# A replanned order for attention with adapters: paired stores, stores cut in unequal parts, and stores that wait on loads

## Chip, core and metric

The kernel runs on one core of a Trainium2 chip. The metric is the device time of one execution in microseconds: 254.63 us as the median of three runs before the change (254.41 to 254.83). The profiled execution took 254.46 us; the program's own span in it is 252.7 us.

## What is computed

Four batches of 6400 rows with 256 channels. First, attention across channels: the 256 x 256 product of normalised k and q over all rows, softmax, and v times the result. Then each row of that result gets a low-rank update from the best 2 of 8 adapters. Cut to what matters:

```python
# q, k, v: (4, 6400, 256) fp32
qn = q / (norm(q, axis=1) + 1e-6);  kn = k / (norm(k, axis=1) + 1e-6)
s = kn.transpose(0, 2, 1) @ qn / tau          # per batch 256 x 256
a = softmax(s);  x = (v @ a).reshape(25600, 256)
logits = x @ w_gate                            # 8 experts
top 2 of the logits, w = softmax of the two
out = x + sum over the two of w * ((x @ A[e]) @ B[e])     # rank 16
```

## The kernel before, in words

**Tiling.** A batch's 6400 rows lie as 128 partitions x 50 columns; one column is 128 rows of 256 fp32. q and k come in pieces of 17, 17 and 16 columns (some cut smaller at the start and in batch 3), v in five pieces of 10 columns, all by GpSimd's queue (L578), which casts to bf16 on the way. The first 4 columns of q and k and the weights come by the queues of SP and ACT. Buffers: 6 pieces of q/k, 3 of v, 4 of transposed v (vT), 7 of output (y), 6 PSUM banks.

**Stages of a batch.** For each column the Gram step G multiplies k by q into the accumulators (L593), and k by k and q by q for the norms (L597, L602). For groups of columns named in OFF the norms go another way: ScalarE squares (L615), VectorE adds (L621), and one small matmul (n2p, L636) sums over partitions. When all 50 columns are in, a chain of small steps follows (norms, rq, s, exp, aT, waA, a), whose end gives the softmax matrix a and a times the gate and A weights. Then each piece of v is transposed (T, L788), and goes through the gate. A piece in MERGED does logits and A product in one matmul group (ZL, L812); the others do logits first (log, L826) and the A product later (Z, L879). gzT (L902) transposes the gated product, Y (L915 and L920) adds v times a and the adapter, Ye (L769 on ScalarE, L771 on VectorE) copies Y out of PSUM into a y piece, and a store (L928) on SP's queue writes the piece. The last two pieces of batch 3 are stored in 4, 4 and 2 columns each.

**Order.** Nothing of the order is left to a scheduler at run time. `make_plan` lists all steps with their engine times, what they need, and what buffers they take and give. `Plan.run` plays them through once at build time with a model of the engines, the TensorE clock and the DMA queues, and the order that comes out is the order of each engine's instructions. WORDS is the order of loads, AHEAD and SQ shift ranks.

**Held stores.** A store of a piece in HOLD does not start before a named load has landed. In this kernel the hold is a small DMA of its own: SP waits for the load, then copies 16 elements into `scrap` (L645), and the stores after it wait on SP's list. SP's list is in order, so a store that waits keeps back all stores behind it, and their y pieces with them.

Of the kernel before, what the change touches and what calls it, by code (L numbers as in the profile page):

```python
# [18 lines left out]
class Step:  # L19
# [3 lines left out]
    def __init__(self, key, eng, deps, rank, take, give, size=0.0):  # L23
        self.packet = max(size, 0.08)
        self.key, self.eng, self.deps, self.rank = key, eng, deps, rank
        self.take, self.give, self.size = take, give, size
        self.users, self.place = [], {}
        self.ready, self.end, self.on = 0.0, None, None
        self.left = len(deps)
        self.only = next(iter(eng)) if len(eng) == 1 else None  # L30


class Clock:


    WINDOW, FIRST, LOW, HIGH = 3.413, 0.31, 0.5, 0.8
# [29 lines left out]
    SPARE = 1.0  # L66


class Plan:

    LAT = 0.07
    DMA_LAT = 1.8
    ENGINES = ("PE", "DVE", "ACT", "POOL", "SP")
    ISSUE = 0.55
    ISSUE_LAT = 1.8
    STORE_LAT = 1.4
    OUT = 8

# [15 lines left out]

    def run(self, head):
# [4 lines left out]
        loads, queue, stores = list(self.loads), [], []  # L100
        now, out, left = 0.0, 0, sum(s.key[0] != "warm" for s in self.steps.values())
        free["POOL"] = 0.2
        clock = Clock()

# [5 lines left out]
        def can_take(s):  # L110
            return all((kind, name) in held or self.store[kind] for kind, name in s.take)

        def start(s, eng):
            for kind, name in s.take:
                if (kind, name) not in held:
                    held[kind, name] = self.store[kind].pop(0)
                    s.place[kind] = held[kind, name]
            s.on = eng
            s.t = now
            self.out.append(s)  # L120

# [5 lines left out]
        while left:  # L127
            again = False
            if (loads and free["POOL"] <= now + 1e-9 and out < self.OUT and can_take(loads[0])):
                s = loads.pop(0)  # L130
                start(s, "POOL")
                out += 1
                free["POOL"] = now + self.ISSUE
                push(free["POOL"], "free", None)
                push(now + self.ISSUE_LAT, "asked", s)
                again = True
            for e in self.ENGINES:
# [3 lines left out]
                for s in wait[e]:  # L141
                    if not can_take(s) or (s.key[0] == "warm" and not clock.idle(now)):
                        continue
# [3 lines left out]
                    if best is None or (s.rank, s.seq) < (best.rank, best.seq):  # L147
                        best = s
# [9 lines left out]
                else:  # L158
                    push(free[e], "end", best)
# [3 lines left out]
            busy = [x for x in (queue, stores) if x]  # L163
            t = events[0][0] if events else float("inf")
            base = max(now, head)

            share = sum(x[0].packet for x in busy)
            if busy:
                t = min(t, base + min(x[0].size / x[0].packet for x in busy) * share)
            assert t < float("inf"), [s.key for s in self.steps.values() if s.end is None][:20]  # L170
            if t > base:
                for x in busy:
                    x[0].size -= (t - base) * x[0].packet / share
                    if x[0].size < 1e-6:
                        push(t + self.DMA_LAT, "landed", x[0])
                        out -= x is queue
                        x.pop(0)
            now = max(now, t)
            while events and events[0][0] <= now + 1e-9:
                _, _, what, s = heapq.heappop(events)  # L180
                if what == "asked":
                    queue.append(s)
                elif what == "store":
                    stores.append(s)
# [3 lines left out]
                elif what == "landed":  # L188
                    push(now + (SAFE if s.on == "POOL" else 0.0), "end", s)
                    for u in s.users:  # L190
                        if u.key[0] == "hold":
                            u.left -= 1
                            if u.left == 0:
                                push(now, "ready", u)
                elif what == "end":
# [6 lines left out]
                    for u in s.users:  # L202
                        u.left -= u.key[0] != "hold"
                        if u.left == 0 and u.eng and u.key[0] != "hold":
                            push(now + (0.0 if s.on == u.only else self.LAT), "ready", u)
# [5 lines left out]
NC = 50  # L211
# [4 lines left out]
V = ((0, 1), (1, 1), (2, 1), (3, 1), (4, 1))  # L216
# [13 lines left out]

def make_plan(B, order, ahead):
# [6 lines left out]
    for kind, b, i in order:  # L238
        if kind == "v":
            p.add(("load", "v", b, i, V[i][0] * PC, V[i][1] * PC), {}, (), 0, take=(("v", (b, i)),),  # L240
                  size=LOAD * V[i][1] * PC + 0.062)
            continue
        for c, n in PARTS.get((b, i), QK[i:i + 1]):
            for h in "qk":
                p.add(("load", h, b, i, c, n), {}, (), 0, take=(("qk", (h, b, i)),), size=LOAD * n + 0.062)

    for h in "qk":
        p.add(("cast", h), {"ACT": 0.6}, [("load", h, 0, 0) + PARTS[0, 0][0]], 0)
    p.loads[2].size += 0.5
    for b in range(B):  # L250

        for i, (c0, n) in enumerate(QK):
            for c in range(c0, c0 + n):
# [8 lines left out]
                p.add(("G", b, c), {"PE": 0.442 - 0.112 * sum((b, group_of(c), w) in OFF for w in "kq")}, deps,  # L262
# [4 lines left out]
        for w in "kq":  # L267
# [5 lines left out]
            for x, g in enumerate(halves):  # L273
                c, n = GROUPS[g]
                i = max(i for i, q in enumerate(QK) if q[0] <= c)
                p.add(("sq", w, b, g), {"ACT": 0.2 + 0.2125 * n},
                      [k for k in p.steps if k[:4] == ("load", w, b, i) and k[4] < c + n and c < k[4] + k[5]]
                      + [("cast", w)] * ((b, c) == (0, 0)), pos["qk", b, i] - SQ, take=(("ssq", (w, b)) if x == 0 else ("sq", (w, b, g)),),
                      give=(("qk", (w, b, i)),))
                if x:  # L280
                    p.add(("add", w, b, g), {"DVE": 0.15 + 0.268 * n},
# [4 lines left out]
            if halves:  # L286
                p.add(("red", w, b), {"DVE": 1.9}, [before], pos["qk", b, len(QK) - 1] - 1, give=(("ssq", (w, b)),))
                p.add(("n2p", w, b), {"PE": 0.35}, [("red", w, b), ("G", b, NC - 3)], -100, take=(("bank", ("n2p", w, b)),))
                late.append(w)
        if b == 0:  # L290
            p.add(("wts",), {"DVE": 1.8}, [("load", "k", 0, len(QK) - 1) + PARTS[0, len(QK) - 1][1]], -200)
# [3 lines left out]
        p.add(("accs", b, 1), {"ACT": 0.38}, [end], ch)  # L295
        p.add(("n2", b, 0), {"DVE": 0.45}, [end], ch)
        p.add(("accs", b, 0), {"ACT": 0.38}, [("n2", b, 0)], ch)
        p.add(("n2", b, 1), {"DVE": 0.45}, [("accs", b, 1)], ch)
        p.add(("rsqrt", b), {"DVE": 1.9 + 0.2 * len(late)},
              [("n2", b, 0), ("n2", b, 1)] + [("n2p", w, b) for w in late], ch, take=(("port", b),),  # L300
              give=(("port", b),) + tuple(("bank", ("n2p", w, b)) for w in late))
        p.add(("rq_ps", b), {"PE": 0.45}, [("rsqrt", b)], ch, take=(("bank", ("rq", b)),))
        for ic in range(2):
            p.add(("s", b, ic), {"DVE": 0.42}, [("rq_ps", b), ("accs", b, ic)], ch, give=(("bank", ("rq", b)),))
            p.add(("exp", b, ic), {"ACT": 0.68}, [("s", b, ic)], ch)
            p.add(("aT_ps", b, ic), {"PE": 0.14}, [("exp", b, ic)], ch, take=(("bank", ("aT", b)),))
        p.add(("recip", b), {"DVE": 0.17}, [("exp", b, 0), ("exp", b, 1)], ch)
        p.add(("aT", b), {"DVE": 0.42}, [("aT_ps", b, 0), ("aT_ps", b, 1)], ch, give=(("bank", ("aT", b)),))
        p.add(("waA_ps", b), {"PE": 0.35}, [("aT", b), ("wts",)], ch, take=(("bank", ("waA", b)),))
        p.add(("waA", b, 0), {"DVE": 0.35}, [("waA_ps", b), ("recip", b)], ch, give=(("bank", ("waA", b)),))  # L310
        p.add(("waA", b, 1), {"ACT": 0.38}, [("waA_ps", b), ("recip", b)], ch, give=(("bank", ("waA", b)),))
        p.add(("a", b), {"DVE": 0.5}, [("recip", b), ("aT", b)] + [("a", b - 1)] * (b > 0), ch + 1)

        for i in range(NP):
            v = max(g for g, (i0, _) in enumerate(V) if i0 <= i)
            x = pos["v", b, v] + 0.3 * (i - V[v][0])
            for u, (c, n) in enumerate(UNITS):
                p.add(("T", b, i, u), {"PE": 0.112 * n + 0.01}, [("load", "v", b, v, V[v][0] * PC, V[v][1] * PC)], x - ahead,
                      take=(("vT", (b, i)), ("bank", ("T", b, i, u))),
                      give=(("v", (b, v)),) if u == len(UNITS) - 1 else ())  # L320
                p.add(("Te", b, i, u), {"DVE": 0.16 + 0.125 * n, "ACT": 0.17 + 0.213 * n},
                      [("T", b, i, u)], x - ahead, give=(("bank", ("T", b, i, u)),))
            merged = (b, i) in MERGED
            if merged:
                for z, (c, n) in enumerate(ZUNITS):
                    p.add(("ZL", b, i, z), {"PE": 0.1145 * n + 0.005},
                          [("Te", b, i, u) for u, (c0, n0) in enumerate(UNITS) if c0 < c + n and c < c0 + n0]
                          + [("waA", b, ic) for ic in range(2)], x - ahead,
                          take=(("bank", ("ZL", b, i, z)), ("zl", (b, i))))
                    p.add(("ZLe", b, i, z), {"ACT": 0.17 + 0.1145 * n, "DVE": 0.14 + 0.142 * n},  # L330
                          [("ZL", b, i, z)], x - ahead, give=(("bank", ("ZL", b, i, z)),))
                prev = [("ZLe", b, i, z) for z in range(len(ZUNITS))]
            else:
                p.add(("log", b, i), {"PE": 0.55},
                      [("Te", b, i, u) for u in range(len(UNITS))] + [("waA", b, ic) for ic in range(2)], x - ahead,
                      take=(("bank", ("log", b, i)), ("gate", (b, i))))
                p.add(("loge", b, i), {"ACT": 0.27, "DVE": 0.27}, [("log", b, i)], x - ahead,
                      give=(("bank", ("log", b, i)),))
                prev = [("loge", b, i)]
            for name, eng, t in (("m1", "DVE", .27), ("eq1", "DVE", .27), ("lm", "DVE", .27),  # L340
                                 ("m2", "DVE", .27), ("msum", "DVE", .19), ("t", "DVE", .27),
# [645 lines left out]
```

## Time and profile before

| | |
|---|---|
| time, median of 3 | 254.63 us |
| span of the profiled execution | 252.7 us |
| TensorE busy | 217.8 us (86%), 2357 matmuls |
| VectorE busy | 192.7 us (76%), 528 instructions |
| ScalarE busy | 151.1 us (60%), 269 instructions |
| DMA packets | 11243 |
| out_dram<-y, 1280 KB each | 18, with 16.7 us from issue to landing |
| v<-in_v_dram, 640 KB each | 20, with 20.5 us from issue to landing |

How to read it: the busy share of an engine is an average over the span; TensorE waits for the first loads early and is full later. The page cuts the span into 40 slices of 6.3 us; in the rows of part 2 each digit is the busy share in tenths, and 9 means 90% or more. A load is counted in bytes as it is written (bf16, so half of what is read), a store as it is (fp32). The time from issue to landing is long because a transfer waits in its queue behind others. The chain that ended last is followed back from the last instruction of the compute engines.

### The profile page before, as it was taken

Reading aid. Unit: us, or ns where it says so; the run is one execution under the profiler, and the core shown is the slowest. Engines: PE = TensorE matmul, PEld = TensorE weight load, DVE = VectorE, ACT = ScalarE, POOL = GpSimd, SP = SyncE. Lnnn points to the kernel's source line nnn. Section 1 sums busy time; section 2 is a strip of 40 time slices with the busy share of each in tenths; the row PEclk is TensorE's granted clock in tenths of the full one; section 3 lists DMA queues with packets and bytes.
Section 4 is the critical chain, followed back from the end, with each engine's and each line's share of the span. In section 5 each row is a group of like instructions: output and inputs, shape, how many; then the busy total and the mean of one; then the engine's idle time right before and its main releaser. Section 6 shows DMA issues by size and latency. Waiting matters only on the chain.

```text
span 252.7 us, 5852 instructions
## 1 busy us (share of the span) xinstructions
PE 217.8 (86%) x2357; PEld 193.0 (76%) x2357; DVE 192.7 (76%) x528; ACT 151.1 (60%) x269; POOL 27.1 (11%) x54
## 2 busy tenths in 40 slices
PE   0274995988999998689999999889999979999990
PEld 0162882876999996579899899779999769999980
DVE  0055589869899987588899899489898898889850
ACT  5454427546786543975667768362674846657671
POOL 7003010040002002000500100500000000000000
PEclk9998899999999999999999999999999999999997
DMA  8999999999999999999999999999999999999996
GB/s 251 217 217 209 211 223 208 217 218 215 215 217 241 303 305 298 224 213 221 210 215 220 215 217 217 211 212 313 317 251 353 322 341 317 337 392 415 404 408 249
DMA packets 11243, 66.70 MB, mean 264 GB/s; under 512 B 1360, under 2 KB 1744, under 8 KB 6608
## 3 DMA queue, kind: packets, MB, share of 16 engines
q0 software_dynamic: 6912, 38.80, 74.4%
q1 hardware_dynamic: 3968, 26.87, 26.1%
q10 hardware_dynamic: 336, 0.66, 0.8%
q8 instruction: 18, 0.29, 0.4%
q14 instruction: 9, 0.07, 0.1%
HBM read 78.91 MB, written 26.21 MB: 416 GB/s over the span
## 4 chain that ended last, share of the span: by engine, by line
PE 53%; DMA 32%; issue 5%; DVE 4%; ACT 2%; POOL 1%; POOLq 0%; DVEq 0%
DMA v<-in_v_dram 18%; PE Y_ps L915 13%; PE acc L593 10%; DMA qk<-in_q_dram 10%; PE Y_ps L920 6%; PE T_ps L788 5%; PE ZL_ps L812 5%; DMA qk<-in_k_dram 5%; PE gzT_ps L902 4%; PE acc L597 3%; PE acc L602 2%; PE Z_ps L879 1%; ACT a_exp L715 1%; DVE a_bf L763 1%; PE log_ps L826 1%
## 5 line engine op out<-in xcount | busy, mean ns | idle before, releaser
L593 PE MATMUL acc<-qk 128*128 128x256 bf16 x400 | 69.6, 282 | 17.0 <-DMA qk<-in_k_dram 9.4
L915 PE MATMUL Y_ps<-a_bf,vT 128*128 128x256 bf16 x400 | 60.0, 273 | 0.2 <-DVE acc_sb L710 0.2
L621 DVE TENSOR_TENSOR ssq<-ssq,sq 128x1280 f32<-128x1280 f32 (+1 forms) x27 | 43.4, 1606 | 19.6 <-ACT sq L615 19.6
L769 ACT COPY y<-Y_ps 128x512 f32<-128x512 f32 x79 | 46.2, 586 | 16.6 <-PE Y_ps L920 13.5
L593 PEld LDWEIGHTS <-qk 128*128 128x128 bf16 x400 | 34.2, 101 | 20.7 <-DMA qk<-in_k_dram 11.5
L615 ACT ACTIVATE sq<-qk 128x1280 f32<-128x1280 bf16 (+1 forms) x27 | 36.9, 1368 | 17.7 <-DVE ssq L621 16.6
L915 PEld LDWEIGHTS <-vT 128*128 128x128 bf16 x400 | 38.9, 98 | 4.7 <-issue 0.3
L920 PE MATMUL Y_ps<-ball,gzT 128*128 128x256 bf16 x200 | 38.2, 273 | 0.0
L597 PE MATMUL acc<-qk 128*128 128x128 bf16 x242 | 34.5, 224 | 0.0
L788 PE MATMUL T_ps<-ident,v 128*128 128x128 f32 x200 | 27.6, 274 | 0.6 <-DVE waA_sb L757 0.4
L769 ACT COPY vT<-T_ps 128x512 f32<-128x512 f32 (+1 forms) x44 | 21.2, 510 | 10.9 <-PE T_ps L788 10.5
L597 PEld LDWEIGHTS <-qk 128*128 128x128 bf16 x242 | 24.4, 101 | 3.5
L890 DVE TENSOR_TENSOR gz<-zl,gateg 128x256 bf16<-128x256 f32 x70 | 26.3, 445 | 0.3
L578 POOL DMA_DIRECT2D v<-in_v_dram x20 | 11.5, 576 | 133.7 <-PE T_ps L788 92.8
L788 PEld LDWEIGHTS T_ps<-ident,v 128*128 128x128 f32 x200 | 22.3, 141 | 1.6 <-DVE waA_sb L757 0.6
L602 PE MATMUL acc<-qk 128*128 128x128 bf16 x168 | 23.4, 222 | 0.0
L902 PE MATMUL gzT_ps<-ident,gz 128*128 128x128 f32 x100 | 20.9, 281 | 2.6 <-DVE gateg L868 1.4
L920 PEld LDWEIGHTS <-gzT 128*128 128x128 bf16 x200 | 19.6, 98 | 2.3
L812 PE MATMUL ZL_ps<-waA_sb,vT 128*128 128x136 bf16 x280 | 19.5, 223 | 1.7 <-DVE waA_sb L757 1.5
L771 DVE COPY gzT<-gzT_ps 128x256 f32<-128x256 f32 (+1 forms) x40 | 15.0, 380 | 7.1 <-PE gzT_ps L902 5.6
L812 PEld LDWEIGHTS <-vT 128*128 128x128 bf16 x280 | 17.7, 98 | 2.4 <-issue 2.1
L615 ACT ACTIVATE ssq<-qk 128x1536 f32<-128x1536 bf16 x8 | 11.9, 1489 | 11.4 <-DMA qk<-in_q_dram 7.4
(80 smaller groups left out, 271.3 us busy)
## 6 DMA issues: line engine op xcount, KB each, us to landing
out_dram<-y SPq DMA_DIRECT2D x18, 1280.0 KB, 16.7
v<-in_v_dram POOLq DMA_DIRECT2D x20, 640.0 KB, 20.5
qk<-in_q_dram POOLq DMA_DIRECT2D x7, 1088.0 KB, 23.7
qk<-in_k_dram POOLq DMA_DIRECT2D x7, 1088.0 KB, 28.4
qk<-in_q_dram POOLq DMA_DIRECT2D x4, 512.0 KB, 19.2
qk<-in_k_dram POOLq DMA_DIRECT2D x4, 512.0 KB, 22.5
qk<-in_q_dram POOLq DMA_DIRECT2D x2, 1024.0 KB, 19.4
qk<-in_k_dram POOLq DMA_DIRECT2D x2, 1024.0 KB, 23.8
```

The lines of the kernel that those rows point to most:

```text
L593: nc.tensor.matmul(acc[ic][:, 0:256], kt[:, j, ic::CC], qt[:, j, :], start=c == 0, stop=False, skip_group_check=True)
L597: nc.tensor.matmul(acc[ic][:, 256:384], kt[:, j, ic::CC], kt[:, j, ic::CC], start=False, stop=False, skip_group_check=True)
L602: nc.tensor.matmul(acc[ic][:, 384:512], qt[:, j, ic * P:(ic + 1) * P], qt[:, j, ic * P:(ic + 1) * P], start=False, stop=c == NC - 1, skip_ ...
L615: nc.scalar.activation(out[:, 0:n, :], t[:, j:j + n, :], ACT.Square)
L621: nc.vector.tensor_tensor(out=t, in0=t, in1=held["sq", (w, b, g), ""][:, 0:n, :], op=OP.add)
L769: nc.scalar.copy(out, in_)
L788: nc.tensor.matmul(ps[:, j, :], vt[:, c + j, :].bitcast(FP32), W["ident32"], is_transpose=True, start=(j == 0), stop=(j == n - 1))
L812: nc.tensor.matmul(ps[:, j, :], vT_of(b, i, c + j)[:, :, ic], st[b]["waA"][:, ic, :], start=(j == 0 and ic == 0), stop=(j == n - 1 and ic ...
L890: nc.vector.tensor_tensor(out=pairs[:, h].rearrange("p c (e r) -> p c e r", e=E), in0=z[:, 2 * h:2 * h + 2, :].rearrange("p c (e r) -> p c ...
L902: nc.tensor.matmul(ps[:, j, :], pairs[:, j * P:(j + 1) * P], W["ident32"], is_transpose=True, start=(j == 0), stop=(j == n // 2 - 1))
L915: nc.tensor.matmul(ps[:, j, :], vT_of(b, i, c + j)[:, :, ic], st[b]["a"][:, ic, :], start=(j == 0 and ic == 0), stop=False, skip_group_che ...
L920: nc.tensor.matmul(ps[:, j, :], pair[:, :, j], W["B"], start=False, stop=(j == 1), skip_group_check=True)
```

## The change

The planner's model of DMA is replaced by one that follows rows through the two queues, one packet at a time, with a fixed part for each row and for the end of a DMA; the step times of nearly all steps are set anew from what executions showed. With it come a new load order (WORDS), new sets OFF, MERGED and HOLD, and new AHEAD, SQ and SAFE. In the emitted program four things are new:

- **Pairs.** Two neighbouring pieces, in PAIRS, share one store of 20 columns. For that all y pieces lie in one tile Y and all v pieces in one tile VS, and a pair takes two places side by side.
- **Stores in four parts.** The store of a piece in SPLIT is issued as four DMAs of 112, 6, 6 and 4 rows, which is meant to spread rows unevenly over the DMA engines.
- **Holds without a DMA.** A held store depends on the load itself; do_hold and its DMA to scrap are gone.
- **Loads of v first.** The first two pieces of v are loaded ahead of batch 1's q and k.

```diff
-V = ((0, 1), (1, 1), (2, 1), (3, 1), (4, 1))
+V = (((0, 1), (1, 1), (2, 1), (3, 1), (4, 1)),) * 4
+PAIRS = {(0, 0), (0, 3), (2, 3)}
...
+def pieces(b, i):
+
+    return next((((b, j), (b, j + 1)) for j in (i - 1, i) if (b, j) in PAIRS), ((b, i),))
...
-    for kind, b, i in sorted(set(HOLD.values())):
-        part = [k for k in p.steps if k[:4] == ("load", kind, b, i)]
-        p.add(("hold", kind, b, i), {"SP": 0.3}, part[-1:], 0, size=0.01)
...
-            parts = UNITS if b == B - 1 and i >= NP - FINE else ((0, PC),)
+            names = pieces(b, i)
+            if (b, i) != names[0]:
+                continue
+            parts = UNITS if b == B - 1 and i >= NP - FINE else ((0, PC * len(names)),)
...
-WORDS = ('q10 v00 v01 v02 q11 v03 q12 v04 v10 v11 q20 v12 v13 v14 q21 v20 v21 v22 q22 q30 '
-         'q31 q32 v23 v24 v30 v31 v32 v33 v34')
-HEAD = 2.6
-LOAD = 0.304
+WORDS = ('v00 v01 q10 v02 q11 q12 v03 v04 v10 v11 q20 v12 q21 q22 v13 v14 v20 q30 q31 v21 v22 q32 v23 v24 v30 '
+         'v31 v32 v33 v34')
+HEAD = 5.05
+COL = 1.024 * 1.17647 / 32
...
-HOLD = {(0, 0): ('k', 3, 1), (0, 1): ('k', 1, 2), (0, 4): ('k', 3, 2), (1, 0): ('k', 3, 1),
-        (1, 1): ('k', 3, 2), (1, 2): ('k', 3, 2), (1, 3): ('k', 3, 2), (1, 4): ('k', 3, 2),
-        (2, 0): ('k', 3, 1), (2, 1): ('k', 3, 2), (2, 4): ('k', 3, 1)}
+HOLD = {(0, 0): ('v', 3, 2), (0, 2): ('v', 0, 1), (0, 3): ('v', 2, 4), (1, 0): ('k', 1, 0), (1, 1): ('v', 2,
+        4), (1, 2): ('v', 2, 1), (1, 3): ('v', 2, 1), (1, 4): ('v', 2, 1), (2, 0): ('v', 0, 2), (2, 1):
+        ('v', 3, 3), (2, 2): ('v', 3, 2), (3, 3): ('k', 2, 1), (3, 4): ('v', 1, 2)}
...
+SPLIT, SHARES = {(1, 1), (2, 4), (3, 0)}, (112, 6, 6, 4)
...
-MERGED = {(0, 1), (0, 2), (0, 3), (1, 0), (1, 1), (1, 2), (1, 3), (1, 4), (2, 0), (2, 1), (2, 2),
-        (2, 4), (3, 2), (3, 4)}
+MERGED = {(0, 0), (0, 4), (1, 0), (1, 3), (2, 0), (2, 1), (2, 2), (3, 0), (3, 1), (3, 2), (3, 4)}
...
     def do_store(s, b, i, c, n):
         lo = i * PC + c
-        nc.sync.dma_start(out_v[b, :, lo:lo + n, :], held["y", (b, i), ""][:, c:c + n, :])
+        at_y = at["y", (b, i)] * PC + c
+        p = 0
+        for rows in SHARES if (b, i) in SPLIT else (P,):
+            r = nc.sync.dma_start(out_v[b, p:p + rows, lo:lo + n, :], Y[p:p + rows, at_y:at_y + n, :])
+            if (b, i) in HOLD and not p:
+                tc.add_manual_dep(r.ins, loaded[held_by(plan, b, i)],
...
+            p += rows
```

OFF names 35 groups before and 43 after. The first four columns of q and k keep their way over SP's and ACT's queues.

## Prediction

> **What bounds the kernel now.** I read the page's part 2 first (the span in 40 slices), then its part 3 (DMA queues), then the windows by stage, then the waits of the store queue, and the chain that ended last only for its end.
>
> ```profile
> PE   0274995988999998689999999889999979999990
> ...
> DMA  8999999999999999999999999999999999999996
> ```
> ```profile
> q0 software_dynamic: 6912, 38.80, 74.4%
> q1 hardware_dynamic: 3968, 26.87, 26.1%
> ...
> HBM read 78.91 MB, written 26.21 MB: 416 GB/s over the span
> ```
> The DMA row has a 9 in every slice but the first and the last, and the queues' shares add to over 100% of 16 engines. Bytes are fixed by the problem: 600 columns of q, k and v read, 200 of output written (a column is 128 x 256 fp32, 131 KB). So the DMA engines are the bound, and TensorE is close behind.
>
> ```profile
> core 0: us, PE busy (x) PEld busy (x) DVE busy (x) ACT busy (x) POOL busy (x), PEclk, DMA share, GB/s
> ...
> 105.00:170.00 65.00, 61.93 (x685) 56.51 (x683) 55.28 (x142) 44.23 (x78) 8.48 (x16) 1.00 1.04 215
> 170.00:204.00 34.00, 33.39 (x392) 30.61 (x389) 30.63 (x95) 20.38 (x45) 1.06 (x2) 1.00 1.04 315
> ...
> 225.00:236.00 11.00, 11.00 (x141) 10.43 (x139) 9.92 (x31) 7.65 (x18) 0.00 (x0) 1.00 1.01 425
> 236.00:247.00 11.00, 10.77 (x103) 9.41 (x101) 6.57 (x22) 7.94 (x16) 0.00 (x0) 1.00 0.97 401
> 247.00:252.70 5.70, 0.00 (x0) 0.00 (x0) 0.00 (x0) 0.39 (x1) 0.00 (x0) 0.69 0.58 229
> ```
> The page counts loads after the cast to bf16, so 215 GB/s of loads alone is 430 GB/s of fp32; 425 is stores alone. Both are the full pace: the loads from 105 to 170 us and the stores from 225 to 236 us leave nothing idle. From 225 to 236 TensorE is busy 11.00 of 11.00 us too. The two lose time only after 236 (0.97) and after 247 (0.58).
>
> ```profile
> 246.55 0.23 PE Y_ps L920 x2
> 246.78 0.02 issue
> 246.81 0.59 ACT y L769
> ```
> ```profile
> SPq L928 <- DVE y L771: 111.6, 6, 73.0
> SPq L645 <- DMA qk<-in_k_dram: 88.7, 3, 76.7
> ...
> SPq L982 <- DMA out_dram<-y: 3.8, 5, 1.2
> ```
> The computed chain ends at 247.40 us, but the last store lands at 251.95. The trace's landing marks say why: a DMA ends with 16 marks[...], and in the last store they run from 249.95 to 251.95. Five engines are within 0.02 us of the first and one is 2.00 us behind. At 242.68 us, with the queue still full, the 16 marks of one store lie at 0, 0.26, 0.36, 0.45, then 0.80 and 1.10, then 1.87 and nine from 2.26 to 3.95: **four engines far ahead, two between, ten behind**. The same spread is 0.65 us at 19 us and 1.78 at 116, so it grows all along. The end is set by the most loaded engine, which never runs dry; the fast ones do, which is the 0.75 of DMA share that the window 238.5 to 240 us shows while the slow ones work on.
>
> [...] loads and stores together (170 to 204 us) have the same 1.04 share as loads alone.
>
> **The change, part by part.**
>
> *Stores cut in four.* SPLIT names pieces (1,1), (2,4) and (3,0), but (2,4) is the second half of the pair (2,3), whose store goes by the name (2,3). The changed kernel's SP list has two such groups of 112, 6, 6, 4 rows, not three. A 10-column store lands 3.04 us after the one before (239.64 to 242.68), and each engine has 8 rows of it, so a row is 0.38 us. [...] Two splits: -0.76 us on ten engines, +0.76 on two, +1.52 on four. [...] the marks above become 1.52 to 1.97 for them, 3.19 at most for the rest, where 3.95 stood: **-0.76 us** on the path that sets the end. That shape (4, 2 and 10 engines) is why I take it. If not, the bounds are +1.52[...] and -0.76. The 6 extra issues cost SP 0.4 to 0.5 us each (the rows of DMA issues take 0.33 and gaps of 0.05 to 0.15 lie between), hidden since a store takes 13.8 us (median) from issue to landing, most of it in the queue.
>
> *Three pairs in one store each.* Three stores fewer. A load of 17 columns takes 5.13 us and a store of 10 takes 3.04; with a fixed part f and g a column, 17g + f = 5.13 and 10g + f = 3.04 give g = 0.2986, f = 0.054. So 3 x 0.054 = **-0.16 us** on every engine; bounds 0 and -0.3.
>
> *The waiting DMAs to scrap (L645) go.* Three on the queue; each puts a 2-byte packet (22 ns by the trace's packets) and a mark (14 ns) on every engine: 3 x 0.036 = **-0.1 us**. In their place a store waits for the landing of a load itself. Behind a waiting store stand all later ones, and behind those the y slots (7) that they free. In the old list, the stores wait for k of batch 3 from 90 to 167 us (longest wait 76.7 us) while loads alone keep the queues full; in the new list they wait for v of (2,1), a load just after k (3,1), so about the same time; then later ones wait for (2,4), (3,2) and (3,3), which lets the last v pieces through at full pace. No cost, as long as loads are queued: there 430 GB/s flow without any store.
>
> *Less mixing.* Mixed stages move 420 to 425 GB/s against 430 (packets summed in 4 us windows), about 1.3 us lost in 80 us of mixing. With two early stores rather than three and pairs of 20 KB rows I take **-0.1 us** (0 to -0.3).
>
> *Norms moved off TensorE.* From the changed list: 322 Gram matmuls of 128 x 128 instead of 410, at 57 ns from start to start: -5.0 us. Three pieces fewer are merged: 60 ZL matmuls less at 59 ns (-3.5), 60 Z more at 56 (+3.4), 60 log more at 25 (+1.5). TensorE: -3.7 us of work, mostly in batches 2 and 3. ScalarE gets 8 squares of 1.37 us (+11), 10 more vT copies (+5) and 17 more gzT copies (+6): 151 to some 175 us. VectorE gets 8 adds of 1.6 us (+13) and gives up about 20 us of copies: 193 to 186. No engine becomes a bound, and since the DMA end does not wait for them this is worth **0 us** by itself; it lets the last Y come some us before 246.8, so that the store queue stays full to the end.
>
> *Order, planner constants, one Y and one v tile.* Same 48 loads, same first ones, so the same start. **0 us**; hidden by the full queues.
>
> Sum: -0.76 - 0.16 - 0.1 - 0.1 = -1.1 us, so 254.63 - 1.1 = **253.5 us**.
>
> **The rivals.**
> 1. [...] Then the extra rows land on an engine that is late: up to +1.52 - 0.36 = +1.2, 255.8 us[...]. Against it: the 4-2-10 shape. For it: nothing names an engine.
> 2. *The new order lets the queues run dry, or TensorE ends later.* After the batch 3 chain the new TensorE list has Y of 8 pieces left, the old one 7: about 3.3 + 0.6 us more work there. If that chain (waA at 203.4 us) does not come earlier, the last Y is at 246.8 + 3.9 = 250.7, the last store 4.5 us behind it at 255.2 instead of 251.95, so 254.63 + 3.3 = 257.9 us; half of that, 256.3. Against it: k (3,2) has landed at 182.9 us already, and the old list still puts all Ys of (2,0) and (2,1) ahead of the last Gram matmuls of batch 3, where the new one has only those of (2,0): the chain can come some 3.3 us earlier, what the eighth piece costs.
> 3. *The balance gains more.* With TensorE done early, no bubble and less mixing, slow engines also lose fewer turns: -0.76 - 0.3 - 0.1 - 0.3 (upper ends) - 0.3 (the bubble near 239 us, 0.25 x 1.5 us, spread over the engines) = -1.8, 252.8 us.
> 4. *Only the small terms hold* (the splits help nine engines but another one, third in the middle group, takes over): -0.36, 254.3 us, no change.
>
> **How the numbers follow.** Forecast 0.55, rival 3 0.18, rival 4 0.11, rival 1 0.07, rival 2 0.09. Faster is forecast and rival 3, 0.73 (253.5 and 252.8 are below 254.12); same 0.12; slower 0.15. The range reaches from 252.5 (rival 3, and bounds of pairs and mixing) to 255.0 (the mild half of rival 1); left out are most of rival 2 and the end of rival 1.
>
> **What would show it.** DMA still 9 in all slices but the ends; the last store's marks spread less than 2 us, or the ends of the ten engines earlier by 0.7; q1 with fewer packets; the last Y well before 246.8 us, and stores the only thing after it. Wrong if a DMA slice falls under 9 in the middle, if TensorE's last Y comes after 248 us, or if the marks of late stores spread over 4 us.

## The result: 257.21 us where 253.5 was forecast, and the profile after

The changed kernel takes 257.21 us (median of 4 runs, 256.77 to 257.78), the kernel before 254.56 beside it: ratio 1.0104, 95% interval 1.0082 to 1.0126. That is 2.65 us slower and outside the range of 252.5 to 255.0. Here and below, times are medians, and a ratio, with its 95% interval, is to the kernel before on the same chip and leaves out runs that lay far above the fastest of their kernel.

Part 2 of the page of the changed kernel, the rows of TensorE, of its granted clock and of DMA, in 40 slices of 6.4 us:

```profile
PE   0682979499999898999999899994998999999980
...
PEclk9976799869999999999999999997799999999996
DMA  8999999999999999999999999999999999999995
```
The DMA row is as full as before. Past the first quarter of the span, new are the 4 in the PE row in slice 28 (172 to 179 us) and two sevens in the clock row, in that slice and the next: TensorE stops, and then runs at less than its full clock.

Part 3 of the same page, the two large queues and the mean over the span:

```profile
q0 software_dynamic: 6912, 38.80, 74.3%
q1 hardware_dynamic: 3472, 26.87, 25.9%
...
HBM read 78.91 MB, written 26.21 MB: 411 GB/s over the span
```
There are 496 packets fewer on the store queue and the same bytes, so 411 GB/s over the longer span where 416 stood. The DMA row doesn't show the loss: its share is as full where less is moved.

The windows of the changed kernel by stage (busy us and count of each engine, granted clock, DMA share, GB/s with loads counted after the cast):

```profile
core 0: us, PE busy (x) PEld busy (x) DVE busy (x) ACT busy (x) POOL busy (x), PEclk, DMA share, GB/s
...
170.00:176.50 6.50, 2.98 (x27) 2.22 (x25) 1.27 (x3) 2.31 (x4) 0.00 (x0) 0.91 1.04 313
176.50:186.00 9.50, 9.49 (x75) 7.59 (x75) 5.40 (x7) 4.97 (x10) 0.00 (x0) 0.70 1.04 268
...
225.00:236.00 11.00, 11.00 (x128) 10.36 (x127) 8.25 (x30) 9.21 (x22) 0.00 (x0) 1.00 1.00 425
236.00:247.00 11.00, 10.90 (x106) 9.49 (x104) 5.81 (x21) 8.23 (x18) 0.00 (x0) 1.00 1.00 403
247.00:256.00 9.00, 1.01 (x10) 0.66 (x7) 0.00 (x0) 1.49 (x3) 0.00 (x0) 0.69 0.59 237
```
From 170 to 176.5 us TensorE works 2.98 of 6.50 us. From 236 to 247 the DMA share is 1.00 instead of 0.97, so by that column no engine runs dry, and yet no more than the 401 GB/s of before are moved.

The last computed step, from the chain that ended last, and the line of the store queue's own waits that took the place of L645:

```profile
248.04 0.59 ACT y L811
```
```profile
SPq L972 <- DMA v<-in_v_dram: 143.5, 5, 76.4
```
The last copy ends 1.2 us later than before (248.63 against 247.40), the last store lands 2.8 us later (254.74 against 251.95). The landing marks show where that begins. A mark is read here as one engine's end of a DMA, which is the author's reading: a whole store leaves 16 in both traces, and the parts of 6, 6 and 4 rows of (3,0) leave one early mark each (228.60 to 229.51) and 6, 6 and 4 as they move. The 112 rows of the cut store (3,0) land at 240.30 with their sixteen marks spread over 1.96 us, 2.66 us after the store ahead of them (237.64): full pace for 7 rows of 0.38 us. Its parts of 6, 6 and 4 rows have landed by 242.35. The whole store behind them, (3,1), lands at 245.41 with a spread of 4.0 us, and the next at 248.46 with 4.05.

The packets of the trace name two places. Up to 184 us both kernels have moved the same bytes to within 0.2 us. By 196 us the changed kernel is behind by bytes worth 1.7 us of DMA time (at 430 GB/s), and by 1.8 us against a version of itself without the stop of TensorE that is shown below. And packets of 10,240 bytes, which take 385 to 398 ns in both kernels, take up to 1,675 ns between 238.8 and 245 us, while from 224 to 238.8 us none takes over 470; before, between 224 and 248 us, four were over 450 ns and the longest took 767.

### The profile page after: what moved, and what is told of

Its sections match the earlier page's. It is cut to its first block, busy times and chain, and to the rows that moved or that the text cites. A ratio compares the mean times of both kernels' runs of the same rounds, so it can differ in the third digit from the quotient of the medians.

```text
span 255.5 us, 5720 instructions
## 1 busy us (share of the span) xinstructions
PE 218.7 (86%) x2306; PEld 190.7 (75%) x2306; DVE 182.0 (71%) x497; ACT 170.0 (67%) x307; POOL 26.3 (10%) x54
## 4 chain that ended last, share of the span: by engine, by line
DMA 39%; PE 38%; DVE 11%; ACT 7%; issue 2%; POOL 1%; POOLq 0%; ACTq 0%
DMA qk<-in_k_dram 28%; PE Y_ps L956 12%; DMA v<-in_v_dram 11%; PE Y_ps L961 6%; PE gzT_ps L943 4%; PE acc L643 4%; PE ZL_ps L853 4%; PE T_ps L829 4%; PE Z_ps L920 3%; DVE ssq L671 2%; ACT y L811 2%; ACT sq L665 2%; DVE ssq L677 2%; ACT zl L811 1%; DVE gz L931 1%
## 5 line engine op out<-in xcount | busy, mean ns | idle before, releaser
L643 PE MATMUL acc<-qk 128*128 128x256 bf16 x400 | 75.3, 286 | 14.8 <-DMA qk<-in_k_dram 8.5
L671 DVE TENSOR_TENSOR ssq<-ssq,sq 128x1280 f32<-128x1280 f32 (+1 forms) x35 | 56.3, 1608 | 29.0 <-ACT sq L665 28.8
L665 ACT ACTIVATE sq<-qk 128x1280 f32<-128x1280 bf16 (+1 forms) x35 | 48.0, 1370 | 22.7 <-DVE ssq L671 8.5
L643 PEld LDWEIGHTS <-qk 128*128 128x128 bf16 x400 | 36.1, 104 | 19.2 <-DMA qk<-in_k_dram 9.8
L956 PEld LDWEIGHTS <-vT 128*128 128x128 bf16 x400 | 39.3, 100 | 8.7 <-issue 3.9
L811 ACT COPY vT<-T_ps 128x512 f32<-128x512 f32 (+1 forms) x54 | 26.5, 532 | 11.0 <-PE T_ps L829 10.5
L652 PE MATMUL acc<-qk 128*128 128x128 bf16 x164 | 23.2, 224 | 0.0
L647 PE MATMUL acc<-qk 128*128 128x128 bf16 x158 | 23.0, 228 | 0.0
L931 DVE TENSOR_TENSOR gz<-zl,gateg 128x256 bf16<-128x256 f32 x55 | 21.2, 448 | 0.1
L811 ACT COPY gzT<-gzT_ps 128x256 f32<-128x256 f32 (+1 forms) x37 | 12.3, 335 | 10.5 <-PE gzT_ps L943 10.4
L811 ACT COPY zl<-ZL_ps 128x408 f32<-128x408 f32 (+1 forms) x32 | 13.2, 451 | 8.5 <-PE ZL_ps L853 8.2
L647 PEld LDWEIGHTS <-qk 128*128 128x128 bf16 x158 | 16.3, 103 | 2.6
L652 PEld LDWEIGHTS <-qk 128*128 128x128 bf16 x164 | 16.0, 101 | 2.1
```

What stands on the lines that cost most here:

```text
L643: nc.tensor.matmul(acc[ic][:, 0:256], kt[:, j, ic::CC], qt[:, j, :], start=c == 0, stop=False, skip_group_check=True)
L647: nc.tensor.matmul(acc[ic][:, 256:384], kt[:, j, ic::CC], kt[:, j, ic::CC], start=False, stop=False, skip_group_check=True)
L652: nc.tensor.matmul(acc[ic][:, 384:512], qt[:, j, ic * P:(ic + 1) * P], qt[:, j, ic * P:(ic + 1) * P], start=False, stop=c == NC - 1, skip_ ...
L665: nc.scalar.activation(out[:, 0:n, :], t[:, j:j + n, :], ACT.Square)
L671: nc.vector.tensor_tensor(out=t, in0=t, in1=held["sq", (w, b, g), ""][:, 0:n, :], op=OP.add)
L811: nc.scalar.copy(out, in_)
```

## The experiments

Theory A: two things cost time. Stores that don't cover all 128 rows are slow while they move, and a square on ScalarE waits for a load with the copies of Y behind it, which stops TensorE and lets the queues run thin. The rivals are that one of the two is all of it, or that the engines that get the extra rows are the late ones. The changed kernel itself was not on the chips of the other runs, so differences from it carry some tenths of a microsecond.

### The wait on ScalarE

ScalarE and TensorE of the changed kernel in time order (start, us, instruction, idle time before it and what ended that):

```profile
169.87 0.37 ACT L811 COPY gzT<-gzT_ps 128x256 f32<-128x256 f32 x1 [0.53 <-PE gzT_ps L943]
174.43 1.48 ACT L665 ACTIVATE sq<-qk 128x1536 f32<-128x1536 bf16 x1 [4.18 <-DMA qk<-in_k_dram]
175.82 2.03 ACT L811 COPY y<-Y_ps 128x512 f32<-128x512 f32 x4
```
```profile
172.62 0.38 PE L643 MATMUL acc<-qk 128*128 128x256 bf16 x2
176.44 1.01 PE L956 MATMUL Y_ps<-a_bf,vT 128*128 128x256 bf16 x4 [3.44 <-ACT y L811]
177.25 0.63 PE L961 MATMUL Y_ps<-ball,gzT 128*128 128x256 bf16 x2
177.67 1.06 PE L956 MATMUL Y_ps<-a_bf,vT 128*128 128x256 bf16 x4
178.53 0.63 PE L961 MATMUL Y_ps<-ball,gzT 128*128 128x256 bf16 x2
178.95 1.06 PE L956 MATMUL Y_ps<-a_bf,vT 128*128 128x256 bf16 x4
```
The square of the first half of k (3,2) stands ahead of four copies of Y on ScalarE's list. It waits 4.18 us for its load. The copies wait with it, they hold the PSUM banks (the matmul accumulators that TensorE writes), and TensorE waits 3.44 us for a bank. After that a group of four and two matmuls takes 1.28 us from start to start (177.67 to 178.95), where the same group takes 0.65 in the kernel with the later square. The plan had that square at 170.97 us. The load's own marks spread over 6.26 us, 168.08 to 174.35; two stores issued at 160.95 and 161.37 us move among the loads in that time, which may be why.

**The square later.**

```diff
     steps = plan.run(HEAD)
+    for late, past in ((("sq", "k", 3, 6), ("Ye", 1, 4, 6)), (("add", "k", 3, 6), ("Ye", 1, 4, 8))):
+        s = next(x for x in steps if x.key == late)
+        steps.remove(s)
+        steps.insert(1 + next(n for n, x in enumerate(steps) if x.key == past), s)
```


> Only the order on two engines changes: ScalarE's square of k's columns 34 to 39 in batch 3, and VectorE's add of it, come after the five copies of Y of piece (1,4) instead of ahead of them. Theory A (the square waits for a late load, keeps back copies that need no load, and TensorE stops for 3.4 us for want of a PSUM bank and then runs 6.8 us at half clock): the stop and the half clock near 175 us are gone, the next v load is issued some 5 us earlier than 186.8, the dip of the queues at 186 to 196 us (1.65 us) is gone, and the time is 257.2 - 1.7 to 2.5 = 254.7 to 255.5 us. Rival H (the held stores leave the queues dry and the stop is beside the point): the dip stays, since stores still wait for v of (2,4), and the time stays within 0.5 us of 257.2. Rival S (the splits set the end): within 0.5 us of 257.2 too, with the dip gone.

Measured: 256.45 us (255.51 to 260.72, six runs), ratio 1.008 (1.0049 to 1.011). ScalarE of this kernel:

```profile
171.10 2.05 ACT L815 COPY y<-Y_ps 128x512 f32<-128x512 f32 x4 [0.62 <-DMA out_dram<-y]
173.99 1.49 ACT L669 ACTIVATE sq<-qk 128x1536 f32<-128x1536 bf16 x1 [0.83 <-DMA qk<-in_k_dram]
```
The copies go first and the square waits 0.83 us. TensorE's stop and the low clock are gone. At 200 us this kernel has moved bytes worth 1.85 us more than the changed one. But the end comes only 0.76 us earlier (the interval of this kernel's own time is 0.8 us to either side): 1.6 us is still the lead at 248 us, and the last engine then needs longer. So the wait is real and, as the next runs show, the smaller part.

### The cut stores in the changed kernel

```diff
-SPLIT, SHARES = {(1, 1), (2, 4), (3, 0)}, (112, 6, 6, 4)
+SPLIT, SHARES = {(1, 1)}, (112, 6, 6, 4)          # one split
+SPLIT, SHARES = set(), (112, 6, 6, 4)             # no split
```


> The changed kernel with the store of (1,1) in four parts and that of (3,0) whole. Landing marks of the changed kernel: 2.0 us of spread from the first split on, 4.0 after the second. Theory B (the second split overshoots[...]): spread stays at 2.0 to 2.3 to the last stores, and the time is 257.2 - 0.8 to 1.2 = 256.0 to 256.4 us. Rival (the forecast's term: each split takes 0.38 us from the most loaded engine): 257.2 + 0.4 = 257.6 us, with spread over 4. Rival (TensorE's last Y sets the end and the balance is hidden): 257.2 within 0.3.

> The changed kernel with all stores whole. Theory B: spread of the landing marks about 4 us with the fast engines ahead, as before the change; the time 257.2 within 0.4, since one right and one overshooting split cancel. The forecast's term: 257.2 + 0.76 = 258.0 us. Rival (the balance is hidden behind TensorE's last Y): 257.2 within 0.3 here and with one split alike.

Measured: one split 255.33 us, ratio 1.0034 (1.0018 to 1.0051); no split 255.12 us, ratio 1.0034 (1.0024 to 1.0044). So the two splits together cost 257.21 - 255.12 = 2.1 us, and nearly all of it is (3,0), 257.21 - 255.33 = 1.9; a cost of (1,1) alone is not resolved. The cut of (1,1) moves at about 205 to 212 us among loads, that of (3,0) from about 236 to 242 us with nothing but stores in the queue.

The marks of the changed kernel show that the last rival is right in part. Those of the first part of 6 rows lie at 239.15, 239.26, 239.57, 239.79, 240.03 and 240.70. Each follows one of the sixteen marks of the 112 rows by 0.37 to 0.40 us, which is one row; those are 238.76, 238.89, 239.19, 239.40, 239.65 and 240.30. So the engine that is first (238.34) carries none of these rows, and one of the two that are last (240.29 and 240.30) does. The part of 4 rows has marks at 240.53, 241.18, 242.00 and 242.35. Eight rows of 0.385 us later are 243.61, 244.26, 245.08 and 245.43, and the store behind has marks at 243.59, 244.25, 245.06 and 245.41, four of its last five. **The engines that carry the part of 4 rows are the late ones behind the cut.** With (3,0) whole, one row behind 240.30 would have ended near 240.7; 242.35 is 1.65 us later. Two more rows at full pace are 0.77 of that (an estimate, 2 x 0.385 us, that takes the last engine to carry a row of all three small parts), and the rest is rows that took longer.

**No split and the square later together**

> The changed kernel with no split store, and with the square of k (3,2) moved behind the copies of Y(1,4) on ScalarE (its add likewise on VectorE). Theory A (splits and ScalarE's wait each cost their own time): the kernel without splits took 255.12 us, the moved square gave 0.76 us; so 254.2 to 254.6 us, no half clock near 175 us, and no dip of the DMA rate at 186 to 196 us. Rival B (without splits the queue makes up for the dip by itself): 254.9 to 255.2 us though the dip is gone. Rival C (the rest of the change gains 0.36 us as forecast once both are out): 254.0 us or less.

Measured: 254.59 us, ratio 1.0003 (0.9995 to 1.0012). From its page, the clock and the group of Y matmuls (busy us, mean ns, idle before):

```profile
PEclk9957699979999999999999999999999999999996
```
```profile
L960 PE MATMUL Y_ps<-a_bf,vT 128*128 128x256 bf16 x400 | 60.0, 273 | 0.1
```
The idle time ahead of these matmuls is 0.1 us; it was 3.5 in the changed kernel. Four kernels now make a square: 257.21 with both, 256.45 with the splits alone, 255.12 with the wait alone, 254.59 with neither. The splits cost 2.1 or 1.9 us, the wait 0.8 or 0.5 (the interval of 256.45 makes one figure of each pair rough), and together they are the whole loss to within 0.3 us. What is left of the change (pairs, holds, order, norms) neither gains nor loses more than that.

**No pairs.** From the kernel just shown, each store of 20 columns is issued as two of 10.

```diff
-            r = nc.sync.dma_start(out_v[b, p:p + rows, lo:lo + n, :], Y[p:p + rows, at_y:at_y + n, :])
+        for x in range(0, n, PC):
+            w = min(PC, n - x)
+            r = nc.sync.dma_start(out_v[b, :, lo + x:lo + x + w, :], Y[:, at_y + x:at_y + x + w, :])
```


> As the kernel with whole stores and the moved square, but each pair of pieces is stored by two stores of 10 columns, issued one after the other where the one of 20 stood. Forecast of the prediction: three stores of 10 more cost 3 x 0.054 = 0.16 us. Rival (a row of 20 KB is no cheaper than two of 10 KB, and the first half of y's places could come free earlier): no difference beyond 0.1 us, or slightly faster.

Measured: 254.63 us, ratio 1.0008 (1.0002 to 1.0015), 0.04 us from the version with pairs. The forecast 0.16 is inside the intervals, and so is zero. A packet of 20,480 bytes takes 761 ns in the median of the kernel with pairs, two of 10,240 take 770 in the one without: there is no large fixed part to save in a row.

### What makes a cut store slow: cuts made in the kernel before

Here the stores (2,2) and (3,0) of the kernel before, which move from about 227 to 240 us with only stores in the queue, are cut in several ways; nothing else changes.

```diff
-        nc.sync.dma_start(out_v[b, :, lo:lo + n, :], held["y", (b, i), ""][:, c:c + n, :])
+        for p in parts if (b, i) in {(2, 2), (3, 0)} else [slice(0, P)]:
+            nc.sync.dma_start(out_v[b, p, lo:lo + n, :], held["y", (b, i), ""][p, c:c + n, :])
```
The variants are the list of parts: 112, 6, 6 and 4 rows; 0-63 and 64-127; even and odd rows; 112 and 16; 112 and four strided fours; 112 alone. The one by columns writes columns 0-4 and 5-9 over all rows. In the expectations, theory P is that it counts which rows go together in a part; P-tail, that only the last 16 rows are slow; P-all, that the part of 112 rows is too; D, that any cut by rows is slow.

> The kernel before the change with nothing new but the stores of (2,2) and (3,0) in parts of 112, 6, 6 and 4 rows. The forecast's term: 254.56 - 0.76 = 253.8 us, spread of the marks from 4.0 down to 3.2. Theory B: the first split brings the spread to about 2, the second back to 4 with other engines last: 254.56 within 0.5. Rival (fewer stores fit among the eight completion semaphores that the stores take in turn, so SP issues later): slower by 0.5 or more, with SP waiting for stores to land.

> The kernel before, with the stores (2,2) and (3,0) issued as rows 0-63 and rows 64-127. [...] Theory P[...]: many of the 10 KB rows of these stores take about twice 385 ns, more than 0.5 us in sum on an engine between 224 and 244 us, and the kernel takes 256 to 260 us. Rival Q (the slow time of the kernel with parts of 112, 6, 6 and 4 comes from rows put on a few engines, or from more DMAs): 254.4 to 254.9 us, and rows of 385 to 400 ns.

> Control for parts: the kernel before, with the stores (2,2) and (3,0) issued as two of 5 columns each over all 128 rows. Theory P: [...] no slow rows, 254.4 to 254.9 us. Rival R (more DMAs in the queue cost time as such, through SP's issues or marks): over 255 us.

> The kernel before, with (2,2) and (3,0) cut in even and odd rows, 64 rows each[...]. [...] Theory P in its simple form[...]: 254.4 to 255 us. Theory D ([...] any other dealing of rows breaks that): 256.5 us or more, rows of 770 ns as in the other halves.

> The kernel before, with (2,2) and (3,0) cut in rows 0-111 and 112-127. [...] Theory P-tail (only the last 16 rows[...] are slow[...]): [...] 255 to 256.9 us. Theory P-all[...]: 257.5 us or more, near the 260.8 of the parts 112, 6, 6, 4. Rival Q (uneven rows or few engines are the cause): 254.4 to 254.9 us.

> The kernel before, with only rows 0-111 of the stores (2,2) and (3,0) written; their last 16 rows are left out (2 x 0.385 us less for each engine). Theory P-all (the part of 112 rows[...] is what costs): 256 us or more, with rows over 700 ns at 228 to 244 us. Theory P-tail (the parts at the end are what costs): 253.7 to 254.3 us, rows of 385 to 400 ns.

> The kernel before, with (2,2) and (3,0) cut in 112 rows and four parts of 4 rows that lie 4 apart. Against the parts of 6, 6 and 4 neighbouring rows (260.83 us) only the choice of the tail's rows differs. Theory P-tail: 254 to 255.5 us. Theory P-all: 257.5 us or more.

| parts of the two stores | us (median) | ratio (95%) | packets over 450 ns, 224 to 248 us | longest, ns |
|---|---|---|---|---|
| whole (the kernel before) | 254.4 | 1 | 4 | 767 |
| two halves by columns | 254.79 | 1.0015 (1.0008 to 1.0021) | 4 | 548 |
| even rows, odd rows | 254.78 | 1.0016 (1.0009 to 1.0022) | 3 | 766 |
| rows 0-63, rows 64-127 | 260.71 | 1.0234 (1.0203 to 1.0265) | 110 | 1361 |
| rows 0-111 alone, rest left out | 257.17 | 1.0107 (1.007 to 1.0145) | 71 | 1668 |
| 112, 16 | 258.16 | 1.0127 (1.0101 to 1.0152) | | |
| 112, 6, 6, 4 | 260.83 | 1.0251 (1.022 to 1.0282) | 92 | 1464 |
| 112, four strided fours | 264.03 | 1.0371 (1.0346 to 1.0397) | 62 | 1536 |

(The packets are those of 10,240 and 5,120 bytes. Of 112 and 16 the one trace is of a run of 262.24 us, so its packets are not read.)

One window of four of these kernels shows it without packets. In order: halves by columns, even and odd rows, rows 0-63 and 64-127, parts of 112, 6, 6 and 4:

```profile
232.00:240.00 8.00, 8.00 (x94) 7.51 (x93) 6.98 (x23) 5.71 (x13) 0.00 (x0) 1.00 1.00 414
```
```profile
232.00:240.00 8.00, 8.00 (x95) 7.52 (x94) 6.98 (x23) 5.71 (x13) 0.00 (x0) 1.00 0.98 410
```
```profile
232.00:240.00 8.00, 8.00 (x95) 7.50 (x93) 6.98 (x23) 5.72 (x13) 0.00 (x0) 1.00 0.99 337
```
```profile
232.00:240.00 8.00, 8.00 (x95) 7.52 (x93) 6.98 (x22) 5.71 (x13) 0.00 (x0) 1.00 1.00 348
```
The compute engines do the same work to 0.02 us and the DMA share is full in all four. The last column differs: 414 and 410 GB/s against 337 and 348. So the share counts an engine as busy while a slow packet is in it.

What follows:

- **Rows 0-63 and 64-127 against even and odd rows** settles most. Both are two DMAs of 64 rows, the same bytes and packet size. Only which rows go together differs, and with it 5.9 us. So neither smaller parts nor more DMAs are needed to lose the time, and theory D falls. Parts on few engines are not needed either: the halves put 4000 packets on the store queue where 3968 stood, 32 for two more DMAs, so each has its 16 marks. That each engine gets the same number of rows of a half is not shown. The rows of a part also decide which addresses in HBM it writes; no run changes the one without the other, so a limit on that side is not excluded.
- Of the 110 packets over 450 ns in the two halves, 44 lie between 740 and 800 ns, about twice the 385 ns of a packet at full pace. With even and odd rows 3 packets are over 450 ns.
- Rows 0-111 alone are slow too, 257.17 us though 16 rows of each store are left out, 0.77 us of moving (an estimate: two rows of 385 ns on each of the 16 engines). What makes a row slow is not shown: these traces name neither the engine of a packet nor what it waits for. They do show rows at half pace outside the cut stores: the last engine needs at least 6.16 us (233.56 to 239.72), 0.77 a row, for the whole store (2,4) at 8 rows an engine, while engines ahead of it already move the 112 rows of (3,0). In the changed kernel, where the engines were closer together, the 112 rows of (3,0) kept their pace; why they did there is open.
- The theory that only the tail of 16 rows can be slow falls. 112 and 16 rows (258.16 us, 1.0127) cost no more, within the noise, than 112 rows alone with the left-out 0.77 us put back (257.17 + 0.77 = 257.9). Put on few engines, the same 16 rows cost more: 1.0251 as 6, 6, 4 and 1.0371 as strided fours. Two things add to the slow rows there.
- The first is which engines carry the small parts. In the kernel with strided fours one engine alone ends 8 us after all the others, and the marks name it: it carries the parts of 4 rows. Those of (2,2) lie at 226.80, 227.01, 227.43 and 229.46, where seven marks of the 112 rows lie from 226.29 to 227.27 and nine from 228.40 to 230.03. Three of the four engines are among those ahead and one among the late; at (3,0) one is 9.1 us behind the first of them (246.43 against 237.34). With parts of 6, 6 and 4 the four marks are 227.56, 228.04, 228.08 and 230.68, again one late.
- The second is the rival named before the run of 112, 6, 6 and 4: stores take eight completion semaphores in turn (in the trace of before, the marks of SP's and ACT's 32 DMAs lie on eight, 64 on each), and with many parts SP waits for a store to land before it issues the next. It is real: the store line waits for landings 5.3 us in all with parts of 6, 6 and 4, and 28.8 us with strided fours, where the DMA share from 232 to 240 us falls to 0.75 and so the engines do run dry. With two parts or one, and in the changed kernel, the store line has no such wait. So it is no cause of the loss there, but the last two rows of the table are not the price of slow rows alone.

### Does the balance itself work?

The kernel with whole stores and the later square, with (1,1) cut, and then (1,1) and (3,0) cut, into 112 rows and four strided fours.

```diff
+        parts = [slice(0, 112)] + [slice(112 + x, P, 4) for x in range(4)] if (b, i) in SPLIT else [slice(0, P)]
+        for p in parts:
+            r = nc.sync.dma_start(out_v[b, p, lo:lo + n, :], Y[p, at_y:at_y + n, :])
```


> The kernel with whole stores and the moved square, and the store (1,1) cut in 112 rows and four parts of 4 rows that lie 4 apart (112, 116, 120, 124; 113, 117, ...)[...] Theory P ([...] the balance itself works): 254.1 to 254.4 us, last store's marks 0.3 us closer. Rival S[...]: 254.6 to 255.5 us.

> As the one before, with (1,1) and (3,0) both cut so. Theory P: 0.77 us less on the ten late engines, 253.8 to 254.2 us. Rival S: the second cut, with only stores in the queue, costs what it cost in the changed kernel: 255.5 to 257 us.

Measured: one cut 254.40 us (253.81 to 255.14), ratio 1.0 (0.9992 to 1.0008); two cuts 259.95 us in the median of six runs that scatter from 256.38 to 260.96, ratio 1.0123 (1.0086 to 1.016). With the one cut among loads, the marks of the last store spread over 3.57 us instead of 3.90, near the 0.3 expected, but the time is not resolved from 254.59 nor from the kernel before. These are single profiles, and the spread moves by more without any cut: it is 0.48 us in the profile with whole stores and the early square, which differs from the one of 3.90 in the place of the square alone. So a fixed number of rows has no fixed lag to even out. The second cut, alone in the queue, costs some 3 us; in its trace the store line waits 6.5 us for earlier stores to land, so this is not the price of slow rows alone. No version tried beats the kernel before.

## Why the prediction was wrong, step by step

**Stores cut in four: -0.76 us forecast, +2.1 (or 1.9) measured. This is the step that failed**, in both of its parts. It put the extra rows on engines that it took to be ahead, and it took a row for 0.38 us on whichever engine carries it. How a cut deals its rows (one row less on ten engines, one more on two, two more on four) was the author's estimate. The count of two groups in the list was right, and the parts of 6 and 4 rows do leave 6 and 4 marks as they move; that the same four engines carry a row of every part is not shown. And of the four engines that carry the part of 4 rows, one is among the late ones in the kernel before, cut in strided fours (229.46 against 226.80 to 227.43), and in the changed kernel one of the last two engines (240.29 and 240.30) gets extra rows. That is rival 1, which the forecast priced at up to +1.2 us and gave 0.07. Nor did the rows keep their 0.38 us when the rows of a DMA were dealt in another way: they took up to 1,675 ns. The bound of +1.52 in the working was a bound on the dealing of rows, not on their price, so the range was too narrow on that side.

**Order and holds: 0 us forecast, +0.5 to +0.8 measured.** This is the second, smaller step that failed. "Hidden by the full queues" held up to 184 us. It left out a wait that the new order adds on ScalarE: a square whose load lands 3.4 us after the plan has the square start, with the copies behind it that free PSUM. Rival 2 had named dry queues, but put them on TensorE's work after the batch 3 chain. TensorE does not set the end: in the kernel with whole stores and the later square its last matmul is done by 244.3 us and the time is 254.59.

**Pairs, scrap holds, less mixing: -0.36 forecast together, +0.16 measured** (254.59 against 254.43 beside it, interval of the ratio -0.13 to +0.31 us). The gain did not show. Of the three only the pairs were tried alone, 0.04 us, not resolved.

**Norms off TensorE: 0 forecast.** They are among what neither gained nor lost, and TensorE did get done early once the wait was gone (8.15 us busy from 236 to 247 us instead of 10.77).

The sum by steps: 2.1 + 0.5 + 0.16 = 2.8 us, against 2.65 measured. Of the three signs that were to show it wrong, no DMA slice in the middle fell under 9; the last Y of TensorE ended at 248.0, on the edge; the spread of late stores did pass 4 us (4.05), but so does that of the kernel before at 230.53 us (4.01), so that sign could not tell the two apart.

## What to carry over

Price a DMA by which rows go together in it, not only by how many rows each engine gets: cut by columns, or into even and odd rows, a store kept its pace here; cut into blocks of rows, it ran at some four fifths of it (337 and 348 GB/s against 414 and 410), with every busy share still full. Before rows are moved to engines that are ahead, look which engines those are: the marks of a part of few rows show it. When a new order puts work that waits for a load ahead of PSUM copies on the same engine, look at the spread of that load's marks, and put the copies first. And judge a full DMA row by the GB/s below it.

## What the runs showed that was not expected

The windows of the changed kernel around TensorE's stop (us, PE busy, granted clock, DMA share, GB/s):

```profile
172.00:176.00 4.00, 1.00 (x9) 0.91 1.04 311
176.00:180.00 4.00, 3.56 (x17) 0.50 1.06 215
```

- After the stop of 3.44 us TensorE's groups took 1.28 us instead of 0.65 until about 182 us. The granted clock shows when: a mean of 0.91 over 172 to 176 us is half clock from about 175.3 on, 2.3 us after the last matmul ended (172.62 + 0.38), and it is 0.50 until 182.1 us, 5.7 us after the next one started (176.44). With the square later there is no such stop, and the clock from 176.5 to 186 us is 1.00 instead of 0.70. The slow matmuls cost some 2.8 us more (an estimate: half of 176.44 to 182.1).
- The same cut cost nothing that is resolved among loads (255.33 against 255.12 us, both at a ratio of 1.0034) and 1.9 us with only stores in the queue; and in the changed kernel's trace no packet of 10,240 bytes takes over 413 ns from 200 to 224 us, where the cut of (1,1) moves.
- A few slow rows don't spread out over the engines. In the two halves, at 244.8 us, the last two marks come 9.0 and 9.1 us after the first, the next at 6.0; in the strided fours one engine, a carrier of the small parts, is 8 us behind all others. Why one alone, and which it is in the two halves, is open.
- Two more DMAs in the queue cost 0.36 and 0.39 us even when no row was slow (columns; even and odd rows). Not explained.
